# Gate and value products of a fused Fourier mixing and ReGLU kernel: two instead of three for eight values, and one gate of six added up in one bank

## The chip, the cores and the metric

The kernel runs on one core of one Trainium2 chip. The metric is device time in microseconds (us), the median of three runs; lower is better. The core has a matrix engine, TensorE (PE), that writes into eight PSUM banks of 128 x 512 floats; VectorE (DVE), ScalarE (ACT) and GpSimd (POOL), which work elementwise, GpSimd on SBUF alone; and SyncE (SP), which here only issues DMAs. Each engine takes its instructions in the order in which the program issues them.

## The reference

Eight sequences of 3,008 tokens with 256 channels go through a two-dimensional Fourier transform, of which the real part is kept, and then through a feed-forward layer with a ReLU gate:

```python
X = np.fft.fft(np.fft.fft(x, axis=1), axis=2).real      # x: 8 x 3008 x 256
t = X.reshape(24064, 256)
gate = np.maximum(t @ w_gate, 0.0)                      # w_gate, w_val: 256 x 1536
out = (gate * (t @ w_val)) @ w_out                      # w_out: 1536 x 256
```

## The kernel before

**Transforms.** The channel transform is multiplied into the weights once: `WA[i]` holds the cosine and `WB[i]` the sine transform of the weights, with i = 0 for the gate and 1 for the value. The sequence transform runs on PE from tables (`dft_steps`, L585) and gives, for each sequence b, a cosine part `U` and a sine part `V` in bfloat16. For a column of `U` and `V`, cosine plus sine product is one token's row, and cosine minus sine product that of the mirrored token. Row 0 of the channel axis needs care: channel 128 is put into row 0 of `V` (`row_0`) and also, spread over all partitions, into `CB` (`row_128`). `WM` is -2 times `WB` with row 0 cleared (`minus_w`).

**Tiles.** A sequence has 1,505 columns, in three blocks of 512, 512 and 481 (`thirds`); the 1,536 hidden units are 12 tiles of 128 (fi 0 to 11). So one sequence makes 36 tiles, written (b, block, fi) here. Sequence 0 has its own code (four segments, `first_tile`, `single_tile`); sequences 1 to 7, 252 tiles, run through `slot`. A tile needs both signs of its gate and its value, and writes relu(gate) x value for each sign into one half of `h`.

**A slot** issues work for four tiles at once: `cur`, the next one `mid`, `nxt` and `after`. For a tile t the steps are:
- three slots ahead, `seed` (L1010, ACT) writes channel 128's share into a bank p, of which there are two;
- two slots ahead, `sine_part` (L1015, PE into the one bank g; L1018, ACT copies it to SBUF as q), `cosine_part` (L1022, PE adds onto the seed), and `both` (L1026, DVE: gate of the plus sign, which is also the last reader of bank p; L1027, GpSimd: gate of the minus sign);
- in its own slot, `value` (L874 and L875, two products into a bank v, of which there are two) and `relu_mult` (L910, DVE: relu(gate) x value, plus sign);
- one slot later, `mirror` (L880, one more product with `WM[1]` onto the same bank, which turns plus into minus) and `second` (L910 again, minus sign).

So a tile takes five products of up to 512 columns. Between these, each slot runs seven or eight output products (L781, 256 columns each) of the block before, five eighths of them ahead of `cosine_part` and the rest at the slot's end. `run_fold` gives GpSimd the folding of the sequence after the next; `run_one(evict)` and `run_one(sums)` give ACT a copy and DVE a half-sum (L597) of a transform. After every sixth slot of the first two blocks, and again two slots later, three transform products run into the one bank d (`DFT_EVEN`); there are none in the third block, and none at all in sequence 7.

**Order on PE** from one `cosine_part` to the next: `cosine_part` of `nxt`, `mirror` of the tile just done, two value products of `cur`, three output products, transform products if any, then in the next slot `sine_part`, four or five output products, `cosine_part`.

**Exceptions.** Tile (1,0,6) is of kind "o": it takes its gate with three products (`gate`, then `mirror`), which makes room for moving in a transform. Tile (1,0,0) is the lead tile, whose slot issues the first output products ahead of `sine_part`. `gate_128` (L833, in slot (2,2) of sequence 0) makes `b2`, the column form of row 0 of `WB[0]`, by twelve products with one column each. `channel_loads` (L133) gathers 3,072 four-byte pieces per load into `CX`, and `keep_rest` (L905) saves the last columns of a 481-column tile by DMA.

Of the kernel before, what the change touches and what calls it, by code (L numbers as in the profile page):

```python
# [11 lines left out]
F32 = mybir.dt.float32  # L12
# [22 lines left out]
def kernel(  # L35
# [27 lines left out]
    def single(name, shape, dt=F32, pool=const):  # L63
        return pool.tile(shape, dt, name=name, tag=name)
# [218 lines left out]
    ums = single("ums", [128, 1])  # L283
    m2 = single("m2", [128, 1])
    half_pi = single("half_pi", [128, 1])
    kvec = single("kvec", [128, NK])
    dvec = single("dvec", [128, 129], pool=st_)
    go = single("go", [128, 2])
    c128p = single("c128p", [128, 2, 3, 2])
# [130 lines left out]
    def weights(c):  # L420

        f = slice(c * 512, (c + 1) * 512)

        def one(i, T, W):
            p = psO.tile([128, 512], F32, name="o", tag="o")
            for kc in range(2):
                nc.tensor.matmul(p[:], lhsT=T[:, kc, :], rhs=wr[i][c][:, kc, :], start=(kc == 0), stop=(kc == 1))
            if (i, c, W) == (0, 1, WA):
                return lambda: nc.scalar.copy(W[i][:, f], p[:])
            if (i, W) in ((1, WA), (c - 1, WB)):  # L430
                nc.vector.tensor_scalar(W[i][:, f], p[:], scalar1=1.0, op0=ALU.mult, scalar2=None)  # L431
            else:
                nc.scalar.copy(W[i][:, f], p[:])
        return [lambda i=i, T=T, W=W: one(i, T, W) for i in range(2) for T, W in ((TA, WA), (TB, WB))]
# [67 lines left out]
            nc.gpsimd.tensor_tensor(FF[0][p, 0, t, :, 0:1], even[:, :, 0:1], even[:, :, 0:1], op=ALU.add)  # L502
    start_pool.__exit__(None, None, None)
    ch128 = nc.dram_tensor("ch128", (B, 4 * NJ + 1), BF16, kind="Internal").ap()
    b2 = single("b2", [128, NF])
    one = single("one", [1, 1], BF16)
    nc.vector.memset(one[:], 1.0)


    def even_table(n, c):  # L510
# [311 lines left out]
    fold_even()  # L822
    turns_and_rows()

    more = {(0, i): [s] for i, s in enumerate(weights(1) + weights(2))}
    for n, c in enumerate(even_order):
        for k, step in enumerate(even_table(n, c)):
            more.setdefault(divmod(EVEN_AT[n] + k, NF), []).append(step)
# [1 line left out]
    for seg in (2, 3):  # L830
        more.setdefault((1, 8 + seg), []).append(lambda seg=seg: minus_v(nc.scalar, seg))

    def gate_128():  # L833
        p = psD.tile([128, 512], F32, name="d", tag="d")
        for f in range(NF):
            nc.tensor.matmul(p[:, f:f + 1], lhsT=WB[0][0:1, f * 128:(f + 1) * 128], rhs=one[:], start=True, stop=True)
        nc.vector.tensor_scalar(b2[:], p[:, 0:NF], scalar1=1.0, op0=ALU.mult, scalar2=None)
    more[(2, 2)] = [gate_128]
    more_1 = {}
    for at, step in zip((-5, -4, -3, -2, -1, 7, 7, 8, 14, 17), channel_loads() + channel_turn()):  # L840
        (more_1 if at >= 0 else more).setdefault(at if at >= 0 else (3, NF + at), []).append(step)

# [8 lines left out]
    def run(todo, n):  # L851
        for _ in range(min(n, len(todo))):
            todo.pop(0)()
        if not paired:
            flush()
# [26 lines left out]
    def bank(tag):  # L882
        return {"g": psG, "p": psP, "v": psV, "d": psD}[tag].tile([128, 512], F32, name=tag, tag=tag)
# [42 lines left out]
    def gate(st, tag="g"):  # L926
        st["g"] = bank(tag)
        two(st["g"], st, 0)
        relu(st)
# [10 lines left out]
    def single_tile(st, outs, extra=(), last=(), tag="p"):  # L940

        gate(st, tag)
        if pending is not None:
            finish(pending)
        value(st)
        mult(st, 0)
        run(todo_out, outs)
        for step in extra:
            step()
        mirror(st["g"], st, 0)  # L950
        relu(st)
        run(todo_out, outs)
        for step in last:
            step()
        return st

    def first_tile(st, extra, outs):
# [31 lines left out]
    def new_tiles():  # L989
        for b in range(1, B):  # L990
            for blk, block in enumerate(thirds):
                for fi in range(NF):
                    st = tile_of(block, fi, uv[b])
                    st["b"] = b
                    st["kind"] = "o" if (b, blk, fi) == (1, 0, 6) else "n"
                    st["lead"] = (b, blk, fi) == (1, 0, 0)
                    yield st

    def prime():
# [4 lines left out]

    def seed(st, p=None):

        if st is None or st["kind"] == "o":
            return
        st["p"] = p or bank("p")
        nc.scalar.activation(st["p"][:, 0:st["n"]], st["c"], ACTF.Copy, scale=b2[:, st["fi"]:st["fi"] + 1])  # L1010

    def sine_part(st):
        n = st["n"]
        st["g"] = bank("g")
        nc.tensor.matmul(st["g"][:, 0:n], lhsT=WM[0][:, st["f"]], rhs=st["vs"], start=True, stop=True)  # L1015
        q = space()
        st["s"] = q, space(), q
        nc.scalar.copy(q[:, 0:n], st["g"][:, 0:n])  # L1018
# [5 lines left out]
    def both(st):  # L1024
        n, (q, sp, sm) = st["n"], st["s"]
        nc.vector.scalar_tensor_tensor(sp[:, 0:n], in0=q[:, 0:n], scalar=-0.5, in1=st["p"][:, 0:n], op0=ALU.mult, op1=ALU.add)  # L1026
        nc.gpsimd.tensor_tensor(sm[:, 0:n], sp[:, 0:n], q[:, 0:n], op=ALU.add)  # L1027

    def slot(cur, mid, nxt, after, outs, fold_us):

        stop = len(todo_out)

        def out(part):
            run(todo_out, len(todo_out) - stop + outs * part // 8)
        old = nxt is not None and nxt["kind"] == "o"
        new = nxt is not None and not old
        if old:
            gate(nxt)
        lead = cur["lead"]
        if lead:  # L1040
            out(5)
        if new and mid["kind"] != "o":
            sine_part(nxt)
        out(3 if not lead else 5)
        out(5)
        if new and mid["kind"] == "o":
            sine_part(nxt)
        if new:
            cosine_part(nxt)
        seed(after)  # L1050
        if pending is not None:
            mirror(pending["v"], pending, 1)
        if pending is not None:
            second(pending)
        value(cur)
        if cur["kind"] == "o":
            mult(cur, 0, cur["first"])
        else:
            relu_mult(cur, 0)
        if new:  # L1060
            both(nxt)
        if old:
            nxt["first"] = nxt["r"]
            mirror(nxt["g"], nxt, 0)
            relu(nxt)
        run_fold(fold_us)
        run_one(evict)
        run_one(sums)
        out(8)
        return cur  # L1070
# [4 lines left out]
    for b in range(B):  # L1075
# [4 lines left out]
        for blk, block in enumerate(blocks):  # L1080
# [44 lines left out]
            if (b, blk) == (0, 0):  # L1125
                for fi in range(NF):
                    st = tile_of(block, fi, (U, V, CB))
                    add_h(st, hs)
                    if fi == 8:
                        todo_out = out_steps(b, block, hs, True)  # L1130
                    pending = first_tile(st, more.get((0, fi), ()), 6)
                mirror(pending["g"], pending, 0)
                relu(pending)
            elif not paired:
                for fi in range(NF):
                    st = tile_of(block, fi, (U, V, CB))
                    add_h(st, hs)
                    tag = {(3, 8): "g", (3, 9): "d", (3, 10): "g", (3, 11): "d"}.get((blk, fi), "p")
                    last = []
                    if (blk, fi) == (3, 11):  # L1140
                        last = [lambda: (sine_part(ahead[1]), cosine_part(ahead[1]), both(ahead[1]), seed(ahead[2]))]
                    if (blk, fi) == (3, 9):
                        ahead = [next(tiles) for _ in range(3)]
                        more[(3, 9)] += [lambda: seed(ahead[0], prime())]
                        more[(3, 10)] += [lambda: seed(ahead[1], prime())]
                        more[(3, 11)] += [lambda: (sine_part(ahead[0]), cosine_part(ahead[0]), both(ahead[0]))]
                    if (blk, fi) == (1, 8):
                        run(todo_out, len(todo_out))
                        todo_out = out_steps(b, block, hs, True)
                    pending = single_tile(st, 3 if blk == 1 else per_tile // 2, more_b.get((blk, fi), ()), last, tag)  # L1150
                    run(todo_dft, DFT_0[blk - 1][fi])
            else:
                for fi in range(NF):
                    at = NF * blk + fi
                    cur = ahead.pop(0)
                    add_h(cur, hs)
                    ahead.append(next(tiles, None))
                    outs = per_tile
                    if (b, blk) == (B - 1, 2) and fi > 8:
                        outs = (10, 11, 17)[fi - 9]  # L1160
                        if fi == 9:
                            rest = out_steps(b, block, hs)
                            early, rest = rest[:10] + rest[12:16], rest[10:12] + rest[16:]
                            todo_out += early
                    pending = slot(cur, *ahead, outs, .72)
                    for step in more_1.get(at, ()) if b == 1 else ():
                        step()
                    run(todo_dft, DFT_1[at] if b == 1 else DFT_EVEN[at])
# [44 lines left out]
```

## Time and profile before

| | us |
|---|---|
| median of three runs (630.84 to 631.08) | 630.92 |
| the profiled execution | 630.98 |
| its span, first to last instruction | 629.2 |
| granted TensorE clock | 1.000 |
| PE: first product starts / last product starts | 1.2 / 625.5 |
| SP held by its longest single issue of L133 | 8.5 |

A line of the profile's groups reads: line of the kernel, engine, operation, tile written <- tiles read, shapes and count; after the bar the busy time in all and the mean of one in ns; after the second bar how long the engine stood idle just before such an instruction, and which instruction of which engine ended most of that. A line of the timeline reads: start, duration, engine, line, operation, tiles, shapes and how many are merged in it; in square brackets the idle time before it and its releaser. The duration of a product on PE goes from its start to its modelled end; products are pipelined, so what a product costs is the distance from its start to the next one's start. DVE and ACT instructions overlap a little too: their starts lie closer than their durations.

### The profile page before, as it was taken

The page shows a single profiled execution, that of the slowest core. Times are in us where ns is not written, and L with a number is a line of the kernel's source. Part 1 is how long each engine was busy: PE and PEld are TensorE (multiplying, and loading weights), DVE is VectorE, ACT ScalarE, POOL GpSimd, SP SyncE. Part 2 cuts the span into 40 slices and gives each one's busy share as a digit, 9 for nine tenths or more (in the row PEclk, how much of TensorE's full clock was granted, in tenths as well). Part 3 has the DMA queues.
Part 4 walks back from the last instruction along what each step waited for, and adds up shares of the span by engine and source line. Part 5 has one row for each costly group of instructions (what it writes and reads, how often), then busy time and mean ns, then how long its engine had stood idle before and what let it go on. Part 6 is the DMA issues. An engine that isn't in the chain of part 4 may idle for free.

```text
span 629.2 us, 12441 instructions
## 1 busy us (share of the span) xinstructions
PE 620.5 (99%) x4114; PEld 398.4 (63%) x4114; DVE 551.5 (88%) x981; ACT 445.5 (71%) x813; POOL 502.7 (80%) x478
## 2 busy tenths in 40 slices
PE   8999999999999999999999999999999999999997
PEld 2566666566666666666666666666666666666666
DVE  8886676999899899988999999899999989999991
ACT  7796667777777767777777777777777777777762
POOL 8887992898999988799979989699886566666660
PEclk9999999999999999999999999999999999999999
DMA  9953748734264327315362426211221111211113
GB/s 240 209 206 118 173 177 102 182 73 151 82 150 145 126 76 183 113 44 165 83 187 64 140 76 130 68 50 36 77 61 38 42 60 56 57 38 51 51 44 102
DMA packets 82911, 66.47 MB, mean 106 GB/s; under 512 B 38517, under 2 KB 65941, under 8 KB 82846
## 3 DMA queue, kind: packets, MB, share of 16 engines
q1 hardware_dynamic: 78260, 60.01, 34.3%
q0 software_dynamic: 3984, 4.92, 3.9%
q10 hardware_dynamic: 602, 0.75, 0.4%
q8 instruction: 32, 0.52, 0.4%
q14 instruction: 33, 0.27, 0.2%
HBM read 41.88 MB, written 34.16 MB: 121 GB/s over the span
## 4 chain that ended last, share of the span: by engine, by line
PE 91%; DVE 4%; issue 2%; POOL 1%; DMA 1%; ACT 1%; DVEq 0%; ACTq 0%; POOLq 0%
PE o L781 36%; PE v L880 10%; PE v L875 9%; PE v L874 9%; PE g L1015 8%; PE p L1022 8%; PE d L585 4%; DVE h L910 2%; PE p L880 1%; PE p L874 1%; PE p L875 1%; DMA XG<-in_x_dram,gidx 1%; DVE h L899 1%; DVE r L1026 1%; POOL XG L120 1%
## 5 line engine op out<-in xcount | busy, mean ns | idle before, releaser
L1027 POOL TENSOR_TENSOR r<-r 128x512 f32<-128x512 f32 (+1 forms) x251 | 313.2, 1254 | 100.5 <-DVE r L1026 98.1
L910 DVE SCALAR_TENSOR_TENSOR h<-r,v 128x512 bf16<-128x512 f32 (+1 forms) x502 | 317.1, 673 | 39.2 <-PE v L880 26.5
L781 PE MATMUL o<-wo,h 128*128 128x256 bf16 x2172 | 330.6, 272 | 0.0
L781 PEld LDWEIGHTS <-h 128*128 128x128 bf16 x2220 | 216.7, 98 | 112.0 <-issue 1.3
L1010 ACT ACTIVATE p<-CB,b 128x512 f32<-128x512 bf16 (+1 forms) x251 | 171.8, 684 | 73.4 <-DVE r L1026 72.1
L1018 ACT COPY r<-g 128x512 f32<-128x512 f32 (+1 forms) x251 | 145.1, 578 | 66.5 <-PE g L1015 57.4
L1026 DVE SCALAR_TENSOR_TENSOR r<-r,p 128x512 f32<-128x512 f32 (+1 forms) x251 | 167.9, 669 | 0.9 <-ACT r L1018 0.9
L875 PE MATMUL v<-V,WB 128*128 128x512 bf16 (+3 forms) x296 | 108.6, 367 | 0.0
L874 PE MATMUL v<-U,WA 128*128 128x512 bf16 (+3 forms) x296 | 108.6, 367 | 0.0
L880 PE MATMUL v<-V,WM 128*128 128x512 bf16 (+1 forms) x252 | 94.4, 375 | 0.8 <-DVE h L910 0.4
L1015 PE MATMUL g<-V,WM 128*128 128x512 bf16 (+1 forms) x251 | 94.1, 375 | 0.5 <-ACT r L1018 0.4
L1022 PE MATMUL p<-U,WA 128*128 128x512 bf16 (+1 forms) x251 | 94.1, 375 | 0.2 <-ACT p L1010 0.2
L899 DVE TENSOR_TENSOR h<-r,v 128x376 bf16<-128x376 f32 (+2 forms) x90 | 46.2, 546 | 17.6 <-PE v L880 10.1
L874 PEld LDWEIGHTS <-WA 128*128 128x128 bf16 x348 | 33.9, 97 | 39.5 <-issue 10.4
L875 PEld LDWEIGHTS <-WB 128*128 128x128 bf16 x348 | 34.0, 98 | 34.3 <-DVE WB L431 0.6
L794 ACT COPY os<-o 128x512 f32<-128x512 f32 x92 | 52.6, 571 | 3.5 <-issue 3.0
L198 POOL TENSOR_TENSOR XG<-XG,XD 128x510 f32<-128x510 f32 x42 | 53.0, 1270 | 0.8 <-DMA XG<-xr 0.8
L890 ACT ACTIVATE r<-p 128x376 f32<-128x376 f32 (+1 forms) x80 | 38.0, 486 | 17.8 <-PE p L880 9.0
L206 POOL TENSOR_TENSOR AA<-XG 128x510 f32<-128x510 f32 x42 | 45.5, 1093 | 0.0
L1015 PEld LDWEIGHTS <-WM 128*128 128x128 bf16 x251 | 24.6, 98 | 5.7 <-issue 0.3
L1022 PEld LDWEIGHTS <-WA 128*128 128x128 bf16 x251 | 24.5, 98 | 3.7 <-issue 0.8
L880 PEld LDWEIGHTS <-WM 128*128 128x128 bf16 x253 | 24.8, 98 | 3.1
(186 smaller groups left out, 412.3 us busy)
## 6 DMA issues: line engine op xcount, KB each, us to landing
out_dram<-os SPq DMA_DIRECT2D x124, 128.0 KB
xr<-in_x_dram SPq DMA_DIRECT2D x12, 768.0 KB
XG<-xr SPq DMA_DIRECT2D x12, 768.0 KB
XD<-in_x_dram SPq DMA_DIRECT2D x15, 512.0 KB
out_dram<-os SPq DMA_DIRECT2D x35, 112.0 KB
XD<-in_x_dram SPq DMA_DIRECT2D x8, 448.0 KB
CB<-ch SPq DMA_DIRECT2D x7, 376.2 KB
out_dram<-os SPq DMA_DIRECT2D x13, 96.0 KB
```

The lines of the kernel that those rows point to most:

```text
L198: e.tensor_tensor(XG[p, r, t, ::-1, 1:D], XG[p, r, t, ::-1, 1:D], XD[p, r, t, :, D - 1:0:-1], op=ALU.add)
L781: nc.tensor.matmul(st["p"][0:m, q, :], lhsT=lhs(f), rhs=wo[:, f, :], start=(f == 0 and not (early and q)), stop=(f == NF - 1), skip_group_ ...
L874: nc.tensor.matmul(bank[:, 0:st["n"]], lhsT=WA[i][:, st["f"]], rhs=st["us"], start=True, stop=False)
L875: nc.tensor.matmul(bank[:, 0:st["n"]], lhsT=WB[i][:, st["f"]], rhs=st["vs"], start=False, stop=True)
L880: nc.tensor.matmul(bank[:, 0:st["n"]], lhsT=W[i][:, st["f"]], rhs=v, start=False, stop=True, skip_group_check=True)
L910: nc.vector.scalar_tensor_tensor(half_h(st, sign), in0=st["s"][1 + sign][:, 0:n], scalar=0.0, in1=st["v"][:, 0:n], op0=ALU.max, op1=ALU.mult)
L1010: nc.scalar.activation(st["p"][:, 0:st["n"]], st["c"], ACTF.Copy, scale=b2[:, st["fi"]:st["fi"] + 1])
L1015: nc.tensor.matmul(st["g"][:, 0:n], lhsT=WM[0][:, st["f"]], rhs=st["vs"], start=True, stop=True)
L1018: nc.scalar.copy(q[:, 0:n], st["g"][:, 0:n])
L1022: nc.tensor.matmul(st["p"][:, 0:n], lhsT=WA[0][:, st["f"]], rhs=st["us"], start=False, stop=True, skip_group_check=True)
L1026: nc.vector.scalar_tensor_tensor(sp[:, 0:n], in0=q[:, 0:n], scalar=-0.5, in1=st["p"][:, 0:n], op0=ALU.mult, op1=ALU.add)
L1027: nc.gpsimd.tensor_tensor(sm[:, 0:n], sp[:, 0:n], q[:, 0:n], op=ALU.add)
```

## The change

The change does the following.

- **Short values.** Eight of the last 48 tiles, fi 4 and 10 of all blocks of sequence 7 and fi 6 and 11 of (6,2), take their value with two products: ACT seeds the transforms' bank d with channel 128's share (`seed_value`), the cosine product adds to it a slot ahead and ACT copies twice the result to SBUF (`value_cosine`), the sine product adds in the tile's own slot (`value_sine`, with `WV`, which is `WB[1]` with row 0 cleared), DVE subtracts to get the minus sign, and GpSimd multiplies it with its gate (`value_second`), on which GpSimd has taken the maximum with 0 in the slot before. `mirror` and `second` fall away for these tiles. A product at slot 26 of sequence 6 sets up bank d.
- **Copied gates.** One gate of six, fi 2 and 8 of every block but (1,0), where it is fi 5 and 9, has no `sine_part` and no `both`. Instead `cosine_part` adds to the seed, ACT copies twice the result to SBUF (`copy_cosine`), a slot later the sine product is added in the same bank (`add_sine`), ACT copies this as the plus sign, and GpSimd subtracts to get the minus sign. In the slot in which a copied tile is `nxt`, `seed(after)` is issued ahead of `cosine_part` and `copy_cosine`; in the next slot `add_sine` is issued behind `sine_part`.
- Tile (1,0,6) becomes an ordinary tile, and the kind "o" goes. In the lead slot, `mirror` and the value come ahead of `cosine_part`.
- **Row 0.** `gate_128` goes. Two DMAs keep row 0 of `WB[0]` and `WB[1]` in DRAM, a third gathers them as 3,072 two-byte pieces, and ACT copies them to `b2`, now 24 columns. After slot 0 of sequence 1 a DMA clears row 0 of `WB[0]`. `weights(2)` moves one slot up. Three ACT passes in sequence 2 make `WV` in the memory of `kvec`.

The core of the diff:

```diff
-    more = {(0, i): [s] for i, s in enumerate(weights(1) + weights(2))}
+    more = {(0, i): [s] for i, s in enumerate(weights(1))}
+    for i, step in enumerate(weights(2)):
+        more.setdefault((0, 3 + i), []).append(step)
...
-    def gate_128():
-        p = psD.tile([128, 512], F32, name="d", tag="d")
-        for f in range(NF):
-            nc.tensor.matmul(p[:, f:f + 1], lhsT=WB[0][0:1, f * 128:(f + 1) * 128], rhs=one[:], start=True, stop=True)
-        nc.vector.tensor_scalar(b2[:], p[:, 0:NF], scalar1=1.0, op0=ALU.mult, scalar2=None)
-    more[(2, 2)] = [gate_128]
-    more_1 = {}
+    def keep_128():
+        for i in range(2):
+            nc.sync.dma_start(out=wrow[i:i + 1], in_=WB[i][0:1, :])
+
+    def get_128():
+        nc.sync.dma_start(out=brow[:], in_=dram(wrow, 0, [[1, 128], [128, 2 * NF]]), allow_slow_non_contiguous=True)
+    more[(1, 1)].append(keep_128)
+    more[(1, 4)].append(get_128)
+    more[(2, 2)] = [lambda: nc.scalar.copy(b2[:], brow[:])]
+    more_1 = {0: [lambda: nc.sync.dma_start(out=WB[0][0:1, :], in_=WM[0][0:1, :])]}
...
+                    st["copied"] = fi in (2, 8) and (b, blk) != (1, 0) or (b, blk, fi) in ((1, 0, 5), (1, 0, 9))
+                    st["short"] = b == 7 and fi in (4, 10) or (b, blk) == (6, 2) and fi in (6, 11)
...
+    def copy_cosine(st):
+        n, sp, sm = st["n"], space(), space()
+        st["s"] = sm, sp, sm
+        nc.scalar.mul(sm[:, 0:n], st["p"][:, 0:n], 2.0)
+
+    def add_sine(st):
+        n, (_, sp, sm) = st["n"], st["s"]
+        nc.tensor.matmul(st["p"][:, 0:n], lhsT=WB[0][:, st["f"]], rhs=st["vs"], start=False, stop=True, skip_group_check=True)
+        nc.scalar.copy(sp[:, 0:n], st["p"][:, 0:n])
+        nc.gpsimd.tensor_tensor(sm[:, 0:n], sm[:, 0:n], sp[:, 0:n], op=ALU.subtract)
+
+    def seed_value(st):
+        st["v"] = bank("d")
+        nc.scalar.activation(st["v"][:, 0:st["n"]], st["c"], ACTF.Copy, scale=b2[:, NF + st["fi"]:NF + st["fi"] + 1])
+
+    def value_cosine(st):
+        n, st["a"] = st["n"], space()
+        nc.tensor.matmul(st["v"][:, 0:n], lhsT=WA[1][:, st["f"]], rhs=st["us"], start=False, stop=True, skip_group_check=True)
+        nc.scalar.mul(st["a"][:, 0:n], st["v"][:, 0:n], 2.0)
+
+    def value_sine(st):
+        n = st["n"]
+        nc.tensor.matmul(st["v"][:, 0:n], lhsT=WV[:, st["f"]], rhs=st["vs"], start=False, stop=True, skip_group_check=True)
+
+    def value_second(st):
+        n = st["n"]
+        a = st["a"][:, 0:n]
+        nc.vector.tensor_tensor(a, a, st["v"][:, 0:n], op=ALU.subtract)
+        nc.gpsimd.tensor_tensor(half_h(st, 1), st["s"][2][:, 0:n], a, op=ALU.mult)
...
+        if nxt is not None and not copied:
+            sine_part(nxt)
+        if mid is not None and mid["copied"]:
+            add_sine(mid)
+        if cur["lead"]:
+            rest_of_pending()
+            value_of_cur()
             out(5)
-        if new and mid["kind"] == "o":
-            sine_part(nxt)
-        if new:
             cosine_part(nxt)
-        seed(after)
...
+        else:
+            out(5)
+            if copied:
+                seed(after)
+                cosine_part(nxt)
+                copy_cosine(nxt)
+            elif nxt is not None:
+                cosine_part(nxt)
+                seed(after)
+            if mid is not None and mid["short"]:
+                value_cosine(mid)
+            rest_of_pending()
+            value_of_cur()
+            if nxt is not None and not copied:
+                both(nxt)
+        if mid is not None and mid["short"]:
+            sm = mid["s"][2][:, 0:mid["n"]]
+            nc.gpsimd.tensor_scalar(sm, sm, scalar1=0.0, op0=ALU.max, scalar2=None)
+        if nxt is not None and nxt["short"]:
+            seed_value(nxt)
```

More of the change, by code (lines that the diff above doesn't have):

```diff
@@ L285 @@
     half_pi = single("half_pi", [128, 1])
-    kvec = single("kvec", [128, NK])
+    kvec = single("kvec", [128, DF // 2])
     dvec = single("dvec", [128, 129], pool=st_)
@@ L504 @@
     ch128 = nc.dram_tensor("ch128", (B, 4 * NJ + 1), BF16, kind="Internal").ap()
-    b2 = single("b2", [128, NF])
-    one = single("one", [1, 1], BF16)
-    nc.vector.memset(one[:], 1.0)
+    wrow = nc.dram_tensor("wrow", (2, DF), BF16, kind="Internal").ap()
+    b2 = single("b2", [128, 2 * NF])
+    brow = single("brow", [128, 2 * NF], BF16)
+    WV = kvec[:].bitcast(BF16)
     def even_table(n, c):
@@ L951, in single_tile @@
         relu(st)
-        run(todo_out, outs)
+        for _ in range(outs):
+            run_one(todo_out)
         for step in last:
             step()
+        run(todo_out, 0)
         return st
@@ L994, in new_tiles @@
                     st["b"] = b
-                    st["kind"] = "o" if (b, blk, fi) == (1, 0, 6) else "n"
                     st["lead"] = (b, blk, fi) == (1, 0, 0)
+                    st["copied"] = fi in (2, 8) and (b, blk) != (1, 0) or (b, blk, fi) in ((1, 0, 5), (1, 0, 9))
+                    st["short"] = b == 7 and fi in (4, 10) or (b, blk) == (6, 2) and fi in (6, 11)
                     yield st
@@ L1005, in seed @@
     def seed(st, p=None):
[L1007 to L1010, printed above, removed]
+        if st is not None:
+            st["p"] = p or bank("p")
+            nc.scalar.activation(st["p"][:, 0:st["n"]], st["c"], ACTF.Copy, scale=b2[:, st["fi"]:st["fi"] + 1])
     def sine_part(st):
@@ L1027, in both @@
         nc.gpsimd.tensor_tensor(sm[:, 0:n], sp[:, 0:n], q[:, 0:n], op=ALU.add)
+    def copy_cosine(st):
[22 more added lines that the diff above has]
+        nc.gpsimd.tensor_tensor(half_h(st, 1), st["s"][2][:, 0:n], a, op=ALU.mult)
+        if n == 481:
+            keep_rest(st)
     def slot(cur, mid, nxt, after, outs, fold_us):
@@ L1034, in out @@
             run(todo_out, len(todo_out) - stop + outs * part // 8)
[L1035 to L1040, printed above, removed]
-            out(5)
-        if new and mid["kind"] != "o":
-            sine_part(nxt)
-        out(3 if not lead else 5)
-        out(5)
-        if new and mid["kind"] == "o":
-            sine_part(nxt)
-        if new:
-            cosine_part(nxt)
@@ L1050, in slot, with rest_of_pending @@
-        seed(after)
[L1051 to L1057, printed above, removed]
-        else:
[L1059 to L1065, printed above, removed]
+        def rest_of_pending():
+            if pending is not None and not pending.get("short"):
+                mirror(pending["v"], pending, 1)
+                second(pending)
@@ new lines, in value_of_cur @@
+        def value_of_cur():
+            if cur["short"]:
+                value_sine(cur)
+            else:
+                value(cur)
+            relu_mult(cur, 0)
+            if cur["short"]:
+                value_second(cur)
+        copied = nxt is not None and nxt["copied"]
+        if cur["lead"]:
+            out(4)
+        if nxt is not None and not copied:
+            sine_part(nxt)
+        if mid is not None and mid["copied"]:
+            add_sine(mid)
+        if cur["lead"]:
+            rest_of_pending()
+            value_of_cur()
+            out(5)
+            cosine_part(nxt)
+            seed(after)
+            both(nxt)
+        else:
+            out(5)
[5 more added lines that the diff above has]
+                cosine_part(nxt)
+                seed(after)
+            if mid is not None and mid["short"]:
[3 more added lines that the diff above has]
+            if nxt is not None and not copied:
+                both(nxt)
@@ L1164 @@
                             todo_out += early
+                    if (b, at) in ((2, 5), (2, 9), (2, 13)):
+                        f = slice(128 * (at - 5), 128 * (at - 1))
+                        nc.scalar.mul(WV[:, f], WM[1][:, f], -0.5)
+                    if (b, at) == (6, 26):
+                        p = bank("d")
+                        nc.tensor.matmul(p[:], lhsT=WA[1][:, 0:128], rhs=U[:, 0:512], start=True, stop=True)
                     pending = slot(cur, *ahead, outs, .72)
```

## The prediction

> **What bounds the kernel now.** I read the page's busy shares first, then the groups, then the timeline.
>
> ```profile
> PE 620.5 (99%) x4114; PEld 398.4 (63%) x4114; DVE 551.5 (88%) x981; ACT 445.5 (71%) x813; POOL 502.7 (80%) x478
> ...
> L1010 ACT ACTIVATE p<-CB,b 128x512 f32<-128x512 bf16 (+1 forms) x251 | 171.8, 684 | 73.4 <-DVE r L1026 72.1
> ```
>
> TensorE (PE) is the bound. The second line is `seed`: ScalarE (ACT) stands idle 72.1 us in all until VectorE (DVE) has done `both` (L1026). This is free today. A quiet stretch of sequence 7, in which no transform runs, shows why:
>
> ```profile
> 575.81 0.68 DVE L1026 SCALAR_TENSOR_TENSOR r<-r,p 128x512 f32<-128x512 f32 x1
> 575.86 0.38 PE L1022 MATMUL p<-U,WA 128*128 128x512 bf16 x1
> ...
> 576.07 0.38 PE L880 MATMUL v<-V,WM 128*128 128x512 bf16 x1
> ...
> 576.52 0.69 ACT L1010 ACTIVATE p<-CB,b 128x512 f32<-128x512 bf16 x1 [0.37 <-DVE r L1026]
> 576.56 1.28 DVE L910 SCALAR_TENSOR_TENSOR h<-r,v 128x512 bf16<-128x512 f32 x2
> ...
> 577.05 0.38 PE L1015 MATMUL g<-V,WM 128*128 128x512 bf16 x1
> ...
> 577.26 0.71 PE L781 MATMUL o<-wo,h 128*128 128x256 bf16 x5
> 577.63 0.58 ACT L1018 COPY r<-g 128x512 f32<-128x512 f32 x1
> ...
> 577.76 0.68 DVE L1026 SCALAR_TENSOR_TENSOR r<-r,p 128x512 f32<-128x512 f32 x1
> 577.81 0.38 PE L1022 MATMUL p<-U,WA 128*128 128x512 bf16 x1
> ...
> 578.48 0.69 ACT L1010 ACTIVATE p<-CB,b 128x512 f32<-128x512 bf16 x1 [0.27 <-DVE r L1026]
> ```
>
> One slot lasts 1.95 us (575.86 to 577.81). Starts are what counts on PE: 0.215 us apart for a 512-column product, 0.109 for an output product, without a gap. Take the seed at 576.52: it waits for `both` (ends 576.49), ends 577.21, and its product is due only at 577.81. So 0.6 us of slack hides the wait.
>
> A stretch with transforms (sequence 3) shows the other state:
>
> ```profile
> 264.59 1.27 DVE L910 SCALAR_TENSOR_TENSOR h<-r,v 128x512 bf16<-128x512 f32 x2
> ...
> 265.79 0.68 DVE L1026 SCALAR_TENSOR_TENSOR r<-r,p 128x512 f32<-128x512 f32 x1
> 265.92 0.38 PE L880 MATMUL v<-V,WM 128*128 128x512 bf16 x1
> ...
> 266.50 0.69 ACT L1010 ACTIVATE p<-CB,b 128x512 f32<-128x512 bf16 x1 [0.57 <-DVE r L1026]
> ...
> 267.13 0.58 ACT L794 COPY os<-o 128x512 f32<-128x512 f32 x1
> ...
> 267.38 0.38 PE L1015 MATMUL g<-V,WM 128*128 128x512 bf16 x1
> ```
>
> Here DVE is late by two half-sums (L597). The `mirror` product at 265.92 starts 0.06 after DVE's pair ends (264.59 + 1.27 = 265.86), and 0.07 after its own turn.
>
> **The change, part by part.** The gain first, on PE:
> - Eight values lose their third product: four of 512 columns at 0.216, four of 481 at 0.203 (304.36 to 304.56 in the timeline): -1.67.
> - `gate_128` goes: twelve one-column products and the wait ahead of them, 64.29 to 64.67 plus 0.10: -0.47.
> - Tile (1,0,6) loses its third gate product (0.22) and the 0.19 that the following `sine_part` waited at 116.20: -0.41.
> - In the lead slot the cosine product waits 0.37 for its seed (106.25). Now `mirror` and the value (0.59) stand ahead of it: -0.37.
> - The extra product that primes the transforms' bank: +0.22.
>
> Together -2.7. Were that all, the time would be 628.3.
>
> **The copied gates, in a quiet slot.** For a copied tile t, `copy_cosine` must have read the bank before `add_sine` may add to it. On ACT the copy is queued behind the seed of tile t+1, and that seed waits for `both` of tile t-1, whose bank it takes over. Put this on the rows, with 575.86 as the cosine product of tile t-1:
> - In the next slot `sine_part` is missing, so the five output products run from 577.05 and the cosine product of t from 577.60. `mirror` would follow at 577.81, but DVE's pair ends at 577.84: it starts at 577.90 (+0.08). Value 578.11 and 578.33, three output products, the sine product of t+1 at 578.87; `add_sine` is due at 579.09.
> - ACT: `both` of t-1 ends 578.44; seed of t+1 at 578.48 as in the row. The next ACT instruction starts 0.63 later (266.50 to 267.13), so the copy runs from 579.11. Its price is that of L1018, 0.585: end 579.69. With 0.05 for the signal `add_sine` starts at 579.74.
>
> It waits 0.65; with the late `mirror` 0.73. I take 0.68, because the 0.08 can shrink when PE has just stood still. Bounds: 0.52 (if the cosine product gained nothing by the missing sine product) and 0.84 (a copy at the seed's 0.69, and the 0.08). Behind `add_sine` on PE stands everything: output products, cosine product, `mirror`, value. No engine can give it back, since PE has no gaps.
>
> Quiet cases: two per sequence in the third block of 1 to 6 (12), six in sequence 7, and tiles (1,0,5) and (1,0,9): 20 x 0.68 = **13.6**.
>
> **In a transform slot.** The slot of a copied tile of blocks 0 and 1 is the one in which three transform products follow. There DVE holds `mirror` at 265.92 whatever PE does before it, so the 0.22 of the missing sine product is lost, and `add_sine` pays 0.22 anew a slot later. The seed is at 266.50, the copy runs 267.13 to 267.71, `add_sine` is due at 267.38 + 0.22 = 267.60 and starts at 267.77: another 0.17. Together 0.39; bounds 0.17 (the 0.22 is given back) and 0.45. 22 cases (two in sequence 1, four in each of 2 to 6): **8.6**.
>
> What copying saves on DVE (a `both`, 0.60 from start to start) is worth nothing: before the half-sums DVE waits for PE anyway, so it can't work ahead.
>
> **The short values.** `value_second` puts 0.60 of DVE ahead of `both`, and the slots of that tile and the next are 0.43 shorter on PE. In sequence 7 the tile four later is a copied one (8 after 4, 2 after 10), whose slot lacks another 0.22; I give the two short tiles of (6,2) the same price. The slack of 0.55 (0.60 less the signal) turns into 0.55 - 0.60 - 0.43 - 0.22 = -0.70: its cosine product waits 0.70 for its seed. DVE catches up meanwhile: its next `both` starts 1.20 (two operations) after the late one, and the waiting cosine product 0.72 + 0.74 after it (`both`, then the seed, with signals). So the next seed starts 1.20 + 0.72 - 1.46 = 0.46 behind that product, the copy ends at 0.46 + 0.63 + 0.585 = 1.67, `add_sine` is due at 1.41 (four products, three output products, one sine product) and waits 0.31, not 0.68. Net 0.70 + 0.31 - 0.68 = 0.33, eight times 2.6, against the 1.67 counted above. Bounds 0 and 5.6.
>
> **Hidden.** GpSimd's added max and product (2.5 us per short tile by the 1.25 of L1027) fit in its idle time, 20.6 us ahead of L1027 between 544 and 600. The gather of 3,072 two-byte pieces has a like in the loads of L133 (3,072 pieces; issued 94.94, packets done by 100). It is queued near 46 and needed near 64: nothing; if that cover fails up to 2. The DMA that clears row 0 of WB0 is issued near 109 and needed near 115: nothing, at most 1. WV's three ACT passes, 0.6 each, meet idle ACT: nothing. `weights(2)` moves by a slot and keeps its instructions: nothing.
>
> **Sum.** 13.6 + 8.6 + 2.6 - 2.7 = +22.1 on the profiled execution's 630.98 (span 629.2 and 1.8 around it), which stands 0.06 above the median 630.92: **653.0**.
>
> **Rivals.**
> - The transform slots swallow theirs (0.17 to none): 630.98 + 13.6 + 2.6 - 2.7 = 644.5. For it: PE has 0.48 of transform products between seed and `add_sine`. Against: `mirror` at 265.92 is DVE's.
> - The copy is in time, and the change is **faster**: 628.3. Place: `add_sine`. Price: nothing but the -2.7. It decides from the point where `both` of t-1 ends 0.65 earlier, at 577.8. Against: that `both` follows two L910 operations that need the previous slot's `mirror` and value, so it cannot.
> - TensorE has idle room into which the waits fall: also 628.3. The rows give 0.215 and 0.109 without gaps, so I give it little. The Trainium skill, Perfetto Trace Analysis, Identifying the Most-Contended Engine, says matmul busy time misjudges the headroom and LDWEIGHTS busy share is to be used. That is 63% here, which would leave room for every wait; the starts in this trace speak against such a reading.
> - Waits build on one another (a late seed delays the next copied tile, 42 x 0.2 more): 661.
>
> **How the numbers follow.** Forecast 0.77, transform slots swallow 0.10, copy in time 0.08, idle room 0.02, compounding 0.03. With the bounds, 20 x 0.52 + 22 x 0.17 = 14.1 less the gains gives 643, and 20 x 0.84 + 22 x 0.45 = 26.7 gives 658 with the short values at their middle. Range 643 to 659. Within 0.2% is about what a measurement of this kernel can't tell from no change: 0.01. Faster 0.09, slower 0.90.
>
> **What would show it.** In the changed kernel's waits, `add_sine` on PE waits for ACT's copy some 42 times, 0.6 quiet and 0.2 in transform slots, 13 to 18 us in all; `mirror`'s waits on L910 (5.2 us in all, added up from the starts in the trace) nearly double; some eight cosine products of sequences 6 and 7 wait 0.7 for seeds. A slot pair around a quiet copied tile lasts 4.6, not 3.9. If `add_sine` follows its sine product after 0.22, the forecast is wrong and the time is near 628.

## The result, and the profile after

| | before | after |
|---|---|---|
| median of four runs, us | 630.95 | 653.04 |
| range of the runs | 630.84 to 631.08 | 652.67 to 653.23 |
| profiled execution / its span | 630.98 / 629.2 | 652.67 / 650.9 |

The change makes the kernel slower: the ratio is 1.0349, with a 95% interval from 1.0331 to 1.0367. The forecast was 653.0.

The page of the changed kernel, with the busy shares, the seed (now L1018) and the two products that wait (`cosine_part` L1030, `mirror` L886):

```profile
PE 627.6 (96%) x4094; PEld 396.5 (61%) x4094; DVE 525.6 (81%) x938; ACT 469.2 (72%) x875; POOL 525.4 (81%) x495
...
L1018 ACT ACTIVATE p<-CB,b 128x512 f32<-128x512 bf16 (+1 forms) x252 | 172.4, 684 | 101.7 <-DVE r L1034 97.9
...
L1030 PE MATMUL p<-U,WA 128*128 128x512 bf16 (+1 forms) x252 | 94.5, 375 | 2.6 <-ACT p L1018 2.6
L886 PE MATMUL v<-V,WM 128*128 128x512 bf16 (+1 forms) x244 | 91.3, 374 | 4.1 <-DVE h L916 1.9
```

VectorE has 26 us less to do than before, and yet the seeds wait for it longer, 97.9 us against 72.1. PE's share fell to 96%, and new idle time stands ahead of its products. In the profile's list of waits the largest of it is

```profile
PE p L1045 <- ACT r L1041: 7.7, 15, 1.5
```

`add_sine` (L1045) waiting for `copy_cosine` (L1041). The line understates it: it counts idle time from the modelled end of the product before, which lies 0.16 behind the point at which the next one could have started, and it holds only 15 of the 42 waits, those over 0.4. I therefore take each product's start less the previous start and less that product's streaming time (0.2158 for 512 columns, 0.2029 for 481, 0.109 for 256: the distances between starts that follow on each other without a gap in these traces), and add up. Here are the waits on PE found in this way, in us, from sequence 1 on, for all kernels of this study. The medians of the lower nine were taken beside runs of the kernel before with medians of 631.16 to 631.22, and their ratios below are to those; so a difference between one of the first two rows and one of the others can be off by 0.2 to 0.3:

| kernel | median | `add_sine` | `mirror` | `cosine_part` |
|---|---|---|---|---|
| before | 630.95 | - | 5.2 | 0.4 |
| after | 653.04 | 15.3 | 11.1 | 3.4 |
| copy ahead of the seed | 638.42 | 0.0 | 11.1 | 4.3 |
| no copied gates | 632.25 | - | 5.8 | 3.2 |
| no short values | 651.76 | 15.8 | 11.9 | 0.0 |
| neither | 630.44 | - | 6.1 | 0.0 |
| no copied gates, subtraction late | 629.75 | - | 6.6 | 0.0 |
| fi 5 and 11, copy first, no short values | 628.31 | 0.0 | 3.7 | 0.2 |
| fi 5 and 11 to sequence 6, copy first, subtraction late | 627.75 | 0.0 | 3.8 | 0.4 |
| fi 3 and 9, copy first | 633.99 | 0.0 | 6.9 | 3.5 |
| fi 3 and 9, seed first | 651.15 | 18.0 | 7.3 | 3.0 |

Before to after, these waits rise by 15.3 + 5.9 + 3.0 = 24.2, products of 1.7 are gone, and `sine_part` waits 0.5 less. That makes 22.0. In the traces, the stretch from the first cosine product of sequence 1 to the last product grew by 21.9; sequence 0 ended 0.8 sooner, and what follows the last product's start took 0.5 longer. The two profiled executions differ by 21.7.

**A quiet slot of the changed kernel** (sequence 5, third block, 481 columns; timeline). The copied tile's cosine product is the one at 474.17:

```profile
474.17 0.37 PE L1030 MATMUL p<-U,WA 128*128 128x481 bf16 x1
474.30 0.65 DVE L1034 SCALAR_TENSOR_TENSOR r<-r,p 128x481 f32<-128x481 f32 x1
...
474.99 0.67 ACT L1018 ACTIVATE p<-CB,b 128x481 f32<-128x481 bf16 x1 [1.22 <-DVE r L1034]
...
475.38 0.37 PE L1023 MATMUL g<-V,WM 128*128 128x481 bf16 x1
...
475.59 0.55 ACT L1041 ACTIVATE r<-p 128x481 f32<-128x481 f32 x1
...
476.19 0.36 PE L1045 MATMUL p<-V,WB 128*128 128x481 bf16 x1 [0.45 <-ACT r L1041]
476.39 0.71 PE L782 MATMUL o<-wo,h 128*128 128x256 bf16 x5
```

Read it from the end. `add_sine` was due 0.20 after the sine product at 475.38, at 475.58; it starts at 476.19, 0.05 after the copy ends (475.59 + 0.55). The copy starts 0.60 after the seed at 474.99, right behind it on ScalarE. The seed starts 0.04 after `both` (474.30 + 0.65 = 474.95), and ScalarE has stood idle for 1.22 us before it, though the cosine product to be copied had its result from about 474.6. The wait is 0.61. The five output products at 476.39 have no wait of their own in the trace and did not pass. The Trainium skill, PSUM — Partial Sum Buffer, Engine vs sequencer instructions, says that matmuls start and complete in program order; this row agrees.

**A transform slot** (sequence 3; timeline):

```profile
269.82 0.38 PE L1030 MATMUL p<-U,WA 128*128 128x512 bf16 x1
...
270.33 0.38 PE L886 MATMUL v<-V,WM 128*128 128x512 bf16 x1
...
271.30 0.64 PE L586 MATMUL d<-tabC,F 128*128 128x376 bf16 x3
271.54 0.58 ACT L1041 ACTIVATE r<-p 128x512 f32<-128x512 f32 x1
271.78 0.38 PE L1023 MATMUL g<-V,WM 128*128 128x512 bf16 x1
...
272.16 0.38 PE L1045 MATMUL p<-V,WB 128*128 128x512 bf16 x1
```

From the cosine product to `mirror` are 0.51 instead of 0.22: `mirror` waits 0.29. At the same place before the change they were 0.29 apart, of which 0.07 was a wait:

```profile
265.63 0.38 PE L1022 MATMUL p<-U,WA 128*128 128x512 bf16 x1
...
265.92 0.38 PE L880 MATMUL v<-V,WM 128*128 128x512 bf16 x1
```

But there the sine product had been done by then. It now follows as `add_sine`, due at 272.00 and started at 272.16, 0.17 late.

### The profile page after: what moved, and what is told of

Read it like the earlier page. It is cut to its first block, busy times and chain, and to the rows that moved or that the text cites. A ratio compares the mean times of both kernels' runs of the same rounds, so it can differ in the third digit from the quotient of the medians.

```text
span 650.9 us, 12420 instructions
## 1 busy us (share of the span) xinstructions
PE 627.6 (96%) x4094; PEld 396.5 (61%) x4094; DVE 525.6 (81%) x938; ACT 469.2 (72%) x875; POOL 525.4 (81%) x495
## 4 chain that ended last, share of the span: by engine, by line
PE 65%; DVE 22%; issue 6%; ACT 4%; DMA 1%; DVEq 0%; SPq 0%; ACTq 0%
PE o L782 23%; DVE h L916 14%; PE v L886 8%; DVE r L1034 6%; PE v L881 6%; PE v L880 6%; PE p L1030 5%; PE g L1023 4%; PE d L586 4%; PE p L1045 2%; ACT r L1041 2%; PE p L886 1%; DMA XG<-xr 1%; PE p L880 1%; PE p L881 1%
## 5 line engine op out<-in xcount | busy, mean ns | idle before, releaser
L916 DVE SCALAR_TENSOR_TENSOR h<-r,v 128x512 bf16<-128x512 f32 (+1 forms) x488 | 309.0, 673 | 86.4 <-PE v L886 77.2
L1035 POOL TENSOR_TENSOR r<-r 128x512 f32<-128x512 f32 (+1 forms) x210 | 262.0, 1251 | 89.7 <-DVE r L1034 87.9
L782 PE MATMUL o<-wo,h 128*128 128x256 bf16 x2172 | 324.8, 272 | 0.0
L1018 ACT ACTIVATE p<-CB,b 128x512 f32<-128x512 bf16 (+1 forms) x252 | 172.4, 684 | 101.7 <-DVE r L1034 97.9
L1026 ACT COPY r<-g 128x512 f32<-128x512 f32 (+1 forms) x210 | 121.7, 579 | 38.5 <-PE g L1023 32.8
L1034 DVE SCALAR_TENSOR_TENSOR r<-r,p 128x512 f32<-128x512 f32 (+1 forms) x210 | 140.5, 669 | 0.6 <-ACT r L1026 0.6
L881 PE MATMUL v<-V,WB 128*128 128x512 bf16 (+3 forms) x288 | 105.6, 367 | 0.0
L880 PE MATMUL v<-U,WA 128*128 128x512 bf16 (+3 forms) x288 | 105.6, 367 | 0.0
L1030 PE MATMUL p<-U,WA 128*128 128x512 bf16 (+1 forms) x252 | 94.5, 375 | 2.6 <-ACT p L1018 2.6
L886 PE MATMUL v<-V,WM 128*128 128x512 bf16 (+1 forms) x244 | 91.3, 374 | 4.1 <-DVE h L916 1.9
L1023 PE MATMUL g<-V,WM 128*128 128x512 bf16 (+1 forms) x210 | 78.8, 375 | 0.1
L905 DVE TENSOR_TENSOR h<-r,v 128x376 bf16<-128x376 f32 (+1 forms) x88 | 44.6, 543 | 17.4 <-PE v L886 8.7
L886 PEld LDWEIGHTS <-WM 128*128 128x128 bf16 x244 | 23.9, 98 | 7.0 <-issue 3.4
L1030 PEld LDWEIGHTS <-WA 128*128 128x128 bf16 x252 | 24.6, 98 | 3.1
```

Source lines behind the costliest of these rows:

```text
L782: nc.tensor.matmul(st["p"][0:m, q, :], lhsT=lhs(f), rhs=wo[:, f, :], start=(f == 0 and not (early and q)), stop=(f == NF - 1), skip_group_ ...
L880: nc.tensor.matmul(bank[:, 0:st["n"]], lhsT=WA[i][:, st["f"]], rhs=st["us"], start=True, stop=False)
L881: nc.tensor.matmul(bank[:, 0:st["n"]], lhsT=WB[i][:, st["f"]], rhs=st["vs"], start=False, stop=True)
L886: nc.tensor.matmul(bank[:, 0:st["n"]], lhsT=W[i][:, st["f"]], rhs=v, start=False, stop=True, skip_group_check=True)
L916: nc.vector.scalar_tensor_tensor(half_h(st, sign), in0=st["s"][1 + sign][:, 0:n], scalar=0.0, in1=st["v"][:, 0:n], op0=ALU.max, op1=ALU.mult)
L1030: nc.tensor.matmul(st["p"][:, 0:n], lhsT=WA[0][:, st["f"]], rhs=st["us"], start=False, stop=True, skip_group_check=True)
```

## The experiments

The theory at the start: the copied gates cost 21 of the 22 us by two separate mechanisms, the copy's place behind the seed (15.3) and the lost 0.22 where VectorE holds `mirror` (5.9); the short values about pay for themselves. The rivals: load on ScalarE, whatever the order; the short values; one cause for both waits.

**1. Copy ahead of the seed.**

```diff
-                seed(after)
                 cosine_part(nxt)
                 copy_cosine(nxt)
+                seed(after)
```

> The changed kernel, but in the slot of a copied gate the seed of the tile after is issued behind the cosine product and its copy. Theory of the queue (the copy is late because it stands behind a seed on ScalarE that waits for VectorE): the 42 waits of add_sine, 15.3 us in the trace of the changed kernel, go, since the copy then ends 1.1 us behind its cosine product and add_sine is due after 1.4; the mirror waits stay (11.1 us against 5.2 before), as they hang on VectorE. 637.7 us. Rival, the transform slots: their waits (3.7 of the 15.3) hang on VectorE's half-sums and stay: 641.4. Rival, load: ScalarE has simply got too much to do (two copies in place of one) and the order is no matter: 653.

Measured: 638.42 us, ratio 1.0116 (1.0100 to 1.0131). All 42 waits of `add_sine` are gone, those of the transform slots too, and the `mirror` waits are as they were. The same slot of sequence 5:

```profile
465.01 0.37 PE L1030 MATMUL p<-U,WA 128*128 128x481 bf16 x1
465.14 0.65 DVE L1034 SCALAR_TENSOR_TENSOR r<-r,p 128x481 f32<-128x481 f32 x1
...
465.48 0.57 ACT L1041 ACTIVATE r<-p 128x481 f32<-128x481 f32 x1 [0.87 <-PE p L1030]
...
465.95 0.66 ACT L1018 ACTIVATE p<-CB,b 128x481 f32<-128x481 bf16 x1
466.22 0.37 PE L1023 MATMUL g<-V,WM 128*128 128x481 bf16 x1
466.42 0.37 PE L1045 MATMUL p<-V,WB 128*128 128x481 bf16 x1
```

The copy now waits for its own product only and ends at 466.05, 0.37 before `add_sine`'s turn; `add_sine` follows its sine product after 0.20, as it should. The seed loses 0.12 (465.95 instead of 465.83, where `both` ends plus 0.04), and its cosine product, at 467.17, has room for that. ScalarE has the same work to do, so load is out as the cause of these waits. The time is 0.7 above the theory's 637.7: the waits at cosine products rose from 3.4 to 4.3, around the two short tiles of (6,2).

**2. No copied gates, 3. no short values, 4. neither.** In `new_tiles`, the first line alone, the second alone, and both:

```diff
+                    st["copied"] = False
+                    st["short"] = False
```

> The changed kernel with no copied gate: all gates by sine_part and both; the short values, the lead slot and the new way of row 0 stay. Theory: copied gates cost 15.3 (add_sine) and 5.9 (more mirror waits); the short values then wait 0.48 each for a seed (0.70 without the missing sine product), 3.1 in all with what they add elsewhere, against 1.67 saved, and the small parts give 1.25: 631.1 us, the same as before. Rival, the short values are what costs (ten or more of the 22): 641 or more.

> The changed kernel with no short value: all values by three products; the copied gates stay as in the change. Theory: 5 waits of 0.70 at cosine products go, 1.3 of longer add_sine waits in (6,2) go, the add_sine waits that the short tiles had shortened to 0.30 are back at 0.61 (5 x 0.31), and 1.67 of products come back: 651.5 us. Rival, the short values cost ten or more: 643 or less.

> The changed kernel with neither copied gates nor short values; the lead slot's order, the ordinary tile (1,0,6), row 0 by DMA and the product that primes the transforms' bank stay. Theory: 0.47 + 0.41 + 0.37 less 0.22 under before: 629.9 us. Rival, the DMAs of row 0 (3,072 two-byte pieces) are late and hold ScalarE in sequence 0: 631.5 or more.

Measured: 632.25 (ratio 1.0016, 1.0007 to 1.0025), 651.76 (1.0326, 1.0310 to 1.0342) and 630.44 (0.9987, 0.9978 to 0.9996). So the copied gates cost 653.04 - 632.25 = 20.8 beside the short values and 651.76 - 630.44 = 21.3 without them. The short values cost 1.3 beside copied gates (1.5 if each time is set against its own runs of the kernel before) and 1.8 without. The small parts together gain 0.8, with an interval of 0.3 to 1.4; the forecast has 1.0. Runs 2 and 4 lie 1.2 and 0.5 above what was expected of them, of which 0.3 is that the kernel before was itself 0.3 higher beside them. Row 0 by DMA is no hindrance.

**5. The subtraction late**, without copied gates:

```diff
             relu_mult(cur, 0)
-            if cur["short"]:
-                value_second(cur)
...
             if nxt is not None and not copied:
                 both(nxt)
+            if cur["short"]:
+                value_second(cur)
```

> As the run without copied gates (632.25), but value_second, the subtraction of a short value on VectorE and its product on GpSimd, is issued behind both of the tile after the next instead of ahead of it. Theory (the short values wait only because 0.60 of VectorE stands between a pair and both, which the next seed awaits): the 7 waits of 0.41 to 0.49 at cosine products go and the eight saved products show in full, 632.25 - 3.2, so 629.1 us. Rival: VectorE has too much to do whatever the order, the wait comes back at mirror: 631.5 to 632.3.

Measured: 629.75 us, ratio 0.9978 (0.9969 to 0.9987). The waits at cosine products go, 3.2 to 0.0, but 0.8 comes back at `mirror`: in sequence 7 it waits 0.14 to 0.16 near each of four short tiles. So both readings hold a part: the place of the subtraction was most of the price, and the rest is VectorE's time. Against the run with neither, the eight saved products of 1.67 bring 0.7.

**6. Copied gates at fi 5 and 11**, copy first as in run 1, no short values:

```diff
+                    st["copied"] = fi in (5, 11)
+                    st["short"] = False
```

> No short values; copied gates at fi 5 and 11 of every block, with the copy ahead of the seed. The slot that lacks sine_part and both is then the one ahead of fi 3 and 9, in which the first half-sum falls. Theory (copying is worth what it takes from VectorE where VectorE is late, and costs where it only moves PE's product): both is missing right ahead of the half-sums, so the mirror waits fall from 6.1 us to some 3.5; 630.44 - 2.3 = 628.1 us. Rival, copied gates cost wherever they stand (ScalarE's second copy): 634 or more, as with fi 2 and 8.

Measured: 628.31 us, ratio 0.9954 (0.9940 to 0.9967). The `mirror` waits fall from 6.1 to 3.7. A copied gate is a gain where it takes `both` from VectorE just ahead of the half-sums that made it late, and its ScalarE copies cost next to nothing in the right order (0.2 at cosine products). In this run's sequence 3, VectorE stands idle for 0.80 behind a half-sum (L598), until a value product is done:

```profile
272.30 0.35 DVE L598 SCALAR_TENSOR_TENSOR U<-es,d 128x188 bf16<-128x188 f32 x1
273.45 1.29 DVE L916 SCALAR_TENSOR_TENSOR h<-r,v 128x512 bf16<-128x512 f32 x2 [0.80 <-PE v L881]
```

**7. Copied gates at fi 5 and 11 up to sequence 6**, copy first as in run 1, short values with the late subtraction of run 5:

```diff
+                    st["copied"] = b < 7 and fi in (5, 11)
```

> Copied gates at fi 5 and 11 of sequences 1 to 6 only, copy ahead of the seed, and the eight short values with the late subtraction. Theory: the gains of the last two runs add up, less what sequence 7 needs none of: 630.44 - 2.3 - 1.3 = 626.8 us, under both kernels. Rival: the two share VectorE's room and do not add: 628.5.

Measured: 627.75 us, ratio 0.9947 (0.9933 to 0.9961): the fastest of all, 3.5 under before. The gains add only in part: the time lies between the theory's 626.8 and the rival's 628.5. Beside run 6 it is 0.6 less, where the short values save 1.67 of products; as this run also takes the copied gates out of sequence 7, the 0.6 isn't theirs alone.

**8. fi 3 and 9, copy first; 9. fi 3 and 9, seed first:**

```diff
+                    st["copied"] = fi in (3, 9) and (b, blk) != (1, 0) or (b, blk, fi) in ((1, 0, 5), (1, 0, 9))
```

> As the run with the copy first (638.42, short values as in the change), but the copied gates are fi 3 and 9 instead of 2 and 8 (in block (1,0) fi 5 and 9 as before), one slot later than the slots whose mirror VectorE holds. Theory (0.22 is lost per copied gate only where mirror waits for VectorE anyway): the growth of the mirror waits from 5.8 to 11.1 us goes: 633 us. Rival, the 5 us belong to copying itself: 638.

> The changed kernel with its order (seed ahead of the copy) but with copied gates at fi 3 and 9, and 5 and 9 in block (1,0). Theory (two separate prices: the seed's place makes add_sine wait; the missing sine product loses 0.22 where VectorE holds mirror): add_sine still waits, some 0.25 in transform stretches and 0.6 in quiet ones, 17 to 19 us in all, and mirror's waits are about those of the run without copied gates (5.8) instead of 11.1: 650 us. Rival, both prices come from the same slot and go together when it is left: 638 or less.

Measured: 633.99 (ratio 1.0046, 1.0031 to 1.0062) and 651.15 (1.0315, 1.0298 to 1.0332). In run 8 the `mirror` waits are 6.9, not 11.1: the growth belonged to the slot, not to copying. In run 9 they are 7.3, while `add_sine` waits 18.0. Two prices, then, that can be taken away one without the other: the order alone gives 14.6 (run 1), the order and the slot 19.0 (run 8), the slot alone 1.9 (run 9), because `add_sine` waits 2.7 more in run 9 than in the changed kernel. Of this, 2.3 fall on the 22 slots of blocks 0 and 1, where no transform products stand between copy and sum any more; the rest is 0.9 more near the short tiles and 0.6 less in one quiet slot. At fi 3 and 9 copying isn't free either: run 8 stands 1.7 above run 2.

## Why the prediction was right

- **The bound.** That PE has no gaps, so that every new wait counts in full, held: 24.2 of waits less 2.2 of products and old waits is 22.0, and the stretch that they lie in grew by 21.9. What showed the bound was the distance between starts. The Trainium skill, Perfetto Trace Analysis, Identifying the Most-Contended Engine, would have us judge TensorE's headroom by MFU (the share of peak FLOP/s) and the LDWEIGHTS busy share. The latter was 63% before and 61% after, and at neither was there room for the waits; MFU was not worked out here.
- **Copied gates, quiet.** Forecast 20 x 0.68 = 13.6. `add_sine` waits 0.60 to 0.61 in the twelve quiet slots of sequences 1 to 6 but one (0.82) and 0.47 twice in block (1,0); in sequence 7 it is 1.68 once, and 0.28 to 0.31 five times behind short tiles. With `mirror` the second quiet slot of a sequence costs 0.61 + 0.07 = 0.68, as forecast. The first costs 0.81, since VectorE is still late there and `mirror` waits 0.30 instead of 0.10. The chain was right.
- **Copied gates, transform slots.** Forecast 22 x 0.39 = 8.6. `add_sine` waits 0.16 to 0.18 in all 22. `mirror` grows by 0.22 in most (0.07 to 0.29, 0.10 to 0.32, 0.21 to 0.43), but not in the first slot of a sequence, where VectorE isn't late (0.05 or 0.16 in all). Quiet and transform slots together are 21.3 by runs 3 and 4, against 22.2 forecast. That what copying saves on VectorE is worth nothing held at fi 2 and 8, for which the prediction worked it out: there copying costs 6.2 even in the right order (run 1 against run 2). At fi 5 and 11 copying gained 2.1 (run 6 against run 4), which the prediction's general wording doesn't allow for.
- **Short values.** Forecast 2.6 of waits against 1.67, net 0.9; measured net 1.3 to 1.5. The makeup differs. Only five cosine products wait, at 0.61 to 0.70: the last short tile has no copied tile behind it. Instead the two short tiles of (6,2), which I gave the same price, make the `add_sine` of two copied tiles wait 0.2 and 1.1 longer, since there the copied tile comes two and three behind and its copy waits for the late `both`. Some 0.4 of the cost is a term that the prediction doesn't have: from the start of the last product to the end of the span are 3.9 to 4.2 in the seven kernels with short values and 3.5 in the three without (3.7 before). Its cause stays open. The longer of the two waits, (7,0,2), with the subtraction (L1065) ahead of `both`:

```profile
562.90 0.65 DVE L1065 TENSOR_TENSOR r<-r,d 128x481 f32<-128x481 f32 x1
...
563.46 0.68 DVE L1034 SCALAR_TENSOR_TENSOR r<-r,p 128x512 f32<-128x512 f32 x1
...
564.18 0.69 ACT L1018 ACTIVATE p<-CB,b 128x512 f32<-128x512 bf16 x1 [1.79 <-DVE r L1034]
...
564.81 0.58 ACT L1041 ACTIVATE r<-p 128x512 f32<-128x512 f32 x1
...
565.43 0.38 PE L1045 MATMUL p<-V,WB 128*128 128x512 bf16 x1 [1.52 <-ACT r L1041]
```

- **Gains.** Forecast 1.03 beside the eight products, measured 0.8 (run 4). In the lead slot `sine_part` waits 0.29 instead of 0.60 and the cosine product not at all, which is more than the 0.37; but `mirror` waits 6.1 instead of 5.2.
- **Hidden work.** The gather is issued at 46.15 and the clearing DMA at 107.72, as thought, and nobody waits for either. GpSimd's maximum takes 1.47, not 1.25, and is hidden too.
- **The rivals.** "The copy is in time" is not what this kernel does, but it is what it does with two lines exchanged (run 1), and even then the time isn't 628.3, as the `mirror` and cosine waits stay. "TensorE has idle room" falls with the bound. "Waits build on one another" isn't seen: the quiet wait is 0.60 to 0.61 in each of the sequences 1 to 5. "The transform slots swallow theirs" falls with the 0.17 and 0.22 in the trace.
- **The sum.** That 653.0 meets 653.04 this closely is luck: copied gates cost 0.9 less than forecast, the short values some 0.5 more, and the small parts gained 0.2 less, so that the misses nearly cancel. The low end of the range is a slip: 630.98 + 14.1 - 2.7 is 642.4, and 645 with the short values, not 643.

What stays open: run 5's 0.8 at `mirror` was read off the trace, but no run took it away. A copied gate in other slots (fi 0, 1, 4) was not tried.

## What to carry to other kernels

On an engine that works in order, an instruction that waits is a gate for all behind it: before putting one that is needed soon behind one that waits for another engine, look up in the timeline when the first one's wait ends. Here exchanging two ScalarE instructions was worth 14.6 us. A wait that costs nothing has slack, and the slack is a number in the trace; shortening the bound engine's slot, or adding to the engine it waits for, eats it from both sides. And what it is worth to take work from an engine that is 88% busy depends on the slot, and of the three places tried it was a gain at one, where the engine had been late: in the right order the same copied gates cost 6.2 us at fi 2 and 8 (run 1 against run 2) and gained 2.1 at fi 5 and 11 (run 6 against run 4).

## What was unexpected of the hardware

GpSimd's maximum with a constant on 128 x 512 floats (L1121) takes longer than its sum of two such tensors (L1035), though it reads half as much. The profile's spans on GpSimd are rough, and no run tells whether it is the constant or something that ran beside it; both instructions write over a tensor that they read. The first line is from the profile's view of L1121, with shortest, median and longest in ns; the second is from the page:

```profile
L1121 POOL TENSOR_SCALAR r<-r x8: 1417/1466/1491, 552.7 to 635.9; 128x481 f32<-128x481 f32 x4, 128x512 f32<-128x512 f32 x4
...
L1035 POOL TENSOR_TENSOR r<-r 128x512 f32<-128x512 f32 (+1 forms) x210 | 262.0, 1251 | 89.7 <-DVE r L1034 87.9
```
